# Routing rounds of a mixture of experts: marks as stationary operand, digits streamed, struck keys kept in place

## The chip, the cores and the metric

One Trainium2 chip, one of its cores. The metric is the device time of one execution in microseconds (us), lower is better. TensorE is called PE here (its weight loads are PEld), VectorE DVE, ScalarE ACT, GpSimd POOL, and SP is the engine that issues most DMAs.

## The reference

Three layers follow each other: attention with pooled queries, a capacity-limited mixture of experts, and a gated feed-forward layer. The change lies in the second one, in the step that assigns each of 2304 tokens to one of 8 experts:

```python
def _moe_ref(x, w_gate, w1, w2):
    N, D = x.shape                     # 2304, 512
    E = w_gate.shape[1]                # 8
    cap = N // E                       # 288
    logits = x @ w_gate
    order = np.argsort(-logits.flatten())
    assigned = -np.ones(N, dtype=np.int64)
    counts = np.zeros(E, dtype=np.int64)
    for idx in order:
        tok, e = int(idx) // E, int(idx) % E
        if assigned[tok] >= 0 or counts[e] >= cap:
            continue
        assigned[tok] = e
        counts[e] += 1
    out = np.zeros((N, D), dtype=np.float32)
    for e in range(E):
        mask = assigned == e
        out[mask] = np.maximum(x[mask] @ w1[e], 0.0) @ w2[e]
    return out
```

All pairs of token and expert are taken from the best logit down; a token takes the first expert that still has room.

## The kernel before

The program has four stages, one after the other: attention (up to about 600 us), the rank of every token within every expert (to about 661 us), the routing (661 to 738 us), and the two feed-forward layers, which keep PE busy to the end. The routing needs the ranks and the preferences, and the first expert needs the routing, since its rows of x are gathered by it. So the routing is a serial piece between two stages that are full.

It works in 7 rounds. A token (i, p) lies at partition p and tile i, with NT = 18 tiles of 128. `key` [128, 18, 8] orders the experts of each token, `Ri` holds its rank in each expert's list. A round does this:

- `choose` and `mark`: each token's best expert that is left (`best`, and `dm`, a 0/1 mark for each token and expert).
- The rank of the chosen pair is split in a high digit (0 to 35, GH = 36) and a low digit (0 to 63, GL = 64). `up_to(k)` writes `ths[k]`, a view of `onehot` [128, 36 or 64, 18] in bfloat16 that holds a 1 where the digit is at most the index. It is written in two halves of 9 tiles.
- `count(0, dm)`: 18 matmuls, one for each tile, add up how many chosen tokens have a high digit up to each value, for each expert. The comparison with the capacity `CAP` (288) gives `inh`, and one matmul with ones turns it into the high digit of the cut, spread over all partitions. `at_cut` and `below` compare each token with it.
- `count(1, at_cut)` does the same for the low digit among tokens at the cut, one more matmul adds those below, and `ind` is the comparison. Two matmuls (`mul64` and `ones64`) give the cut as a rank, spread over all partitions.
- `cutb` keeps the lowest cut of each expert so far; the next round's `allowed` compares `Ri` with it (`ok`) and multiplies `key` by that into `s1`, from which the round chooses.

In `count`, the digits are the stationary operand (a slice `ths[k][:, :, i]`, so its columns lie 18 bfloat16 or 36 bytes apart), and the marks are streamed (`who[:, i, :]`, 8 columns side by side); the counts lie by digit, 36 or 64 partitions of 8 values. After a round's last matmul PE transposes four blocks of x for a row tile that ACT scales and SP stores (`rows_after`, six rounds), and then does six matmuls into `acc`, whose result nobody reads (`warm3`, 512 columns each). In this stage the order within an engine is the order of the code, but for what stands under `issue_after`, which waits behind the named instruction. PE, DVE and ACT take their instructions strictly in that order here; a wait is a semaphore.

Of the kernel before, what the change touches and what calls it, by code (L numbers as in the profile page):

```python
# [113 lines left out]
def fused_attention_moe_kernel(ctx: ExitStack, tc: tile.TileContext,  # L114
# [28 lines left out]
    PRM = {'vdue': 6, 'e0': 24, 'egap': 34, 'stag': 6, 'edue': -4, 'rdue': -3, 'plo': -6, 'phi': -8, 'xdue': 3, 'mdue': -10, 'pool': 0, 'vp': (3, 3, 3, 3), 'tok': 1, 'kdue': 2, 'k2due': 2, 'sdue': 0, 'cdue': 40, 'ldma': 1, 'warm': 1, 'warm2': 5, 'warm3': 6, 'nact': (1, 7, 10, 13, 16), 'adel': 2, 'kpref': 5, 'dve': (0, 1, 1, 1), 'edve': (0, 0, 1, 1), 'eat': (1, 4, 7, 9), 'dendue': 10, 'u1due': 0, 'pw': (40, 4, 20, 4), 'tord': 6, 'cmul': 1.35, 'ldlat': 6.0, 'stlat': 6.0, 'eoff': 8, 'espan': 36,  'swn': (3, 3, 3, 3), 'swdue': 2, 'mlo': 2, 'mhi': -8, 'ehold': 16}  # L143
# [1007 lines left out]
    ind = sm("ind", [GL, E], BF)  # L1151
    inh = sm("inh", [GL, E], BF)
    HT = NT // 2

    def choose(src):
        nc.vector.tensor_reduce(best, src, axis=AX.X, op=OP.max)

    def mark(src):
        return nc.vector.tensor_tensor(dm, src, best[:, :, None].to_broadcast([128, NT, E]), op=OP.is_equal)

    def allowed():
        nc.vector.tensor_tensor(ok, Ri, cutb[:, None, :].to_broadcast([128, NT, E]), op=OP.is_lt)
        nc.vector.tensor_mul(s1, ok, key)
        return s1
# [28 lines left out]
    src = key  # L1193
    for rnd in range(E - 1):
        if rnd:
# [5 lines left out]
        p = count(0, dm, GH)  # L1201
# [430 lines left out]
```

## Time and profile before

| | before |
|---|---|
| median of 3 runs | 1428.38 us (1425.8 to 1432.29) |
| the profiled execution | 1425.41 us, of it 1423.6 us from the first to the last instruction |
| PE busy | 1338.2 us, 94% of the span |
| DVE busy | 932.2 us, 65% |
| ACT busy | 612.3 us, 43% |
| POOL busy | 522.6 us, 37% |

The busy shares are means over stages that differ. The routing is some 5% of the span, and PE, which is full before and behind it, has a lower granted clock there. What an edit of the routing is worth is therefore read from one round: which engine each step waits for, and how long.

### The profile page before, as it was taken

The numbers are of one execution on the slowest core, as the hardware profiler recorded it, in microseconds if no ns is written. First come the engines' busy times: TensorE is split into PE (matmuls) and PEld (weight loads), VectorE is DVE, ScalarE is ACT, GpSimd is POOL, SyncE is SP. The second block draws the span as 40 slices with busy tenths as digits, with TensorE's granted clock in tenths as the row PEclk, the third lists the DMA queues.
The fourth block names the chain that finished last, engine by engine and source line by source line (L and its number), as shares of the span: only waits on it lengthen the run. The fifth ranks groups of instructions, "written<-read, shape, count | busy, mean of one in ns | idle before, by whom it ended". The sixth has DMA issues, their size and how long they took to land.

```text
span 1423.6 us, 26934 instructions
## 1 busy us (share of the span) xinstructions
PE 1338.2 (94%) x10278; PEld 1108.9 (78%) x10279; DVE 932.2 (65%) x1940; ACT 612.3 (43%) x1643; POOL 522.6 (37%) x447
## 2 busy tenths in 40 slices
PE   7999999999999888787889999999999999999997
PEld 5666655666665777686669999999999999999997
DVE  5657679878989899878548888866742323232322
ACT  4456555555545565465115555654421212121211
POOL 7545323433324364553027767755610000000000
PEclk9899999999989999887569999999999999999999
DMA  7566566566633886621027767764310101010000
GB/s 221 153 180 182 145 156 184 148 179 190 174 87 87 217 187 158 153 76 53 30 87 239 239 210 254 261 205 128 90 45 1 45 1 45 1 45 1 23 1 23
DMA packets 78353, 174.45 MB, mean 123 GB/s; under 512 B 8448, under 2 KB 38160, under 8 KB 78224
## 3 DMA queue, kind: packets, MB, share of 16 engines
q1 hardware_dynamic: 75248, 163.29, 40.6%
q0 software_dynamic: 2976, 9.44, 1.8%
q8 instruction: 81, 1.33, 0.4%
q14 instruction: 48, 0.39, 0.1%
HBM read 120.86 MB, written 21.31 MB: 100 GB/s over the span
## 4 chain that ended last, share of the span: by engine, by line
PE 61%; issue 17%; DVE 14%; ACT 3%; POOL 2%; DMA 2%; SPq 1%; POOLq 0%; ACTq 0%; DVEq 0%
PE pv L385 8%; PE py L1442 7%; PE ph L1423 7%; PE st L351 6%; DVE cmp L561 5%; PE pg L1529 5%; PE misc L1529 5%; PE po L1552 5%; PE pm L282 4%; PE st L352 3%; PE pv L400 2%; DVE cmp L563 2%; PE pc L1177 2%; PE csum L1224 1%; DVE cmp L993 1%
## 5 line engine op out<-in xcount | busy, mean ns | idle before, releaser
L294 DVE TENSOR_REDUCE mxp<-pm 128x1 f32<-128x384 f32 x405 | 199.6, 549 | 74.4 <-PE pm L282 71.2
L373 ACT ACTIVATE Lrow<-st 128x288 f32<-128x288 f32 (+2 forms) x432 | 154.4, 411 | 95.4 <-PE st L352 82.4
L351 PE MATMUL st<-qs,ks 128*128 128x288 f32 (+2 forms) x504 | 172.7, 354 | 9.8 <-ACT Lrow L373 5.7
L352 PE MATMUL st<-qs,ks 128*128 128x288 f32 (+2 forms) x504 | 150.8, 309 | 3.1 <-ACT qs L333 2.9
L561 DVE SCALAR_TENSOR_TENSOR cmp<-Lrow,Lt,cmp 128x384 fp8e4<-128x384 f32 (+8 forms) x145 | 152.7, 1073 | 0.0
L1560 POOL DMA_INDIRECT out_dram<-ot,si x18 | 17.5, 971 | 362.4 <-DVE ot L1557 359.8
L393 POOL TENSOR_TENSOR Lrow<-Lrow 128x576 f32<-128x576 f32 (+2 forms) x50 | 70.4, 1408 | 204.5 <-ACT Lrow L373 201.9
L1540 DVE TENSOR_TENSOR sg<-pg,sg 128x384 f32<-128x384 f32 x72 | 40.1, 557 | 159.4 <-ACT sg L1539 159.4
L351 PEld LDWEIGHTS st<-qs,ks 128*128 128x128 f32 x504 | 100.0, 198 | 49.3 <-ACT Lrow L373 22.9
L385 PE MATMUL pv<-Lrow,v 128*64 128x288 f32 (+2 forms) x900 | 125.4, 416 | 3.4 <-ACT den L422 3.2
L1339 POOL TENSOR_TENSOR wl<-wr,wh 128x512 fp32r<-128x512 f32 x67 | 104.5, 1567 | 59.8 <-ACT wh L1337 28.9
L352 PEld LDWEIGHTS st<-qs,ks 128*128 128x128 f32 x504 | 101.3, 201 | 4.7 <-ACT qs L333 4.7
L1539 ACT ACTIVATE sg<-pg 128x384 f32<-128x384 f32 x72 | 35.3, 491 | 155.4 <-PE pg L1529 155.4
L1542 ACT CAST ah<-ac 128x384 fp32r<-128x384 f32 x72 | 36.9, 513 | 149.2 <-DVE ac L1541 149.2
L1529 PE MATMUL pg<-yh,w2h 128*128 128x384 f32 x288 | 97.0, 337 | 0.0
L1529 PE MATMUL pg<-yl,w2h 128*128 128x384 f32 x288 | 96.9, 337 | 0.0
L1529 PE MATMUL pg<-yh,w2l 128*128 128x384 f32 x288 | 96.8, 336 | 0.0
L1529 PE MATMUL misc<-yh,w2h 128*128 128x384 f32 x288 | 96.8, 336 | 0.0
L1529 PE MATMUL misc<-yl,w2h 128*128 128x384 f32 x288 | 96.8, 336 | 0.0
L1529 PE MATMUL misc<-yh,w2l 128*128 128x384 f32 x288 | 96.8, 336 | 0.0
L385 PEld LDWEIGHTS pv<-Lrow,v 128*64 128x64 f32 x900 | 59.4, 140 | 46.8 <-issue 13.8
L1552 PE MATMUL po<-w2l,ah 128*128 128x512 f32 x216 | 85.5, 396 | 0.0
(285 smaller groups left out, 3490.2 us busy)
## 6 DMA issues: line engine op xcount, KB each, us to landing
wr<-in_wm_dram SPq DMA_DIRECT2D x64, 512.0 KB, 3.6
raw<-in_wm_dram SPq DMA_DIRECT2D x36, 512.0 KB, 4.5
ks<-pkh SPq DMA_DIRECT2D x23, 576.0 KB, 5.6
v<-in_v_dram SPq DMA_DIRECT2D x20, 576.0 KB, 6.3
pk<-in_kT_dram SPq DMA_DIRECT2D x16, 576.0 KB, 5.3
pq<-in_qT_dram SPq DMA_DIRECT2D x32, 288.0 KB, 5.8
Lrow<-l_cols SPq DMA_DIRECT2D x18, 512.0 KB, 5.4
ks<-kh_s SPq DMA_DIRECT2D x16, 576.0 KB, 7.0
```

What stands on the lines that cost most here:

```text
L294: nc.vector.tensor_reduce(mx[:, i, j:j + 1], p[:, :w3], axis=AX.X, op=OP.max)
L351: nc.tensor.matmul(p[:, :w], KS[u][:, 1, ks], QS[u][:, 1, cs_], start=True, stop=False)
L352: nc.tensor.matmul(p[:, :w], KS[u][:, 0, ks], QS[u][:, 0, cs_], start=False, stop=True)
L373: nc.scalar.activation(EX[u, gi, kt][:, ti * w:(ti + 1) * w], ST.pop((u, gi, kt, ti))[:, :w], AF.Exp, scale=SCALE)
L385: nc.tensor.matmul(p[64 * k:64 * k + 64, :hn], VT[u][:, kt, o:o + 64], ex[:, k * hn:(k + 1) * hn], start=(kt == 0), stop=(kt == KT - 1), s ...
L393: nc.gpsimd.tensor_add(w[:, :n], a, b)
L561: nc.vector.scalar_tensor_tensor(c[:, sl], Lrow[:, e, sl], Lt[:, i, e:e + 1], c[:, sl], op0=OP.is_ge, op1=OP.add, accum_out=acc, saturate= ...
L1339: eng.tensor_sub(WL[k][:, s], r[:, s], WH[k][:, s].bitcast(F32))
L1423: nc.tensor.matmul(p[:, :CAP], w[:, cs_], x[:, c, :], start=(n == 0), stop=(n == 11))
L1442: nc.tensor.matmul(PY[e][m][:, :CAP], w[:, ms], h, start=(f == 0 and n == 0), stop=(f == FB1 - 1 and n == 2))
L1529: nc.tensor.matmul(p[:, :TG], w[ft][:, cs_], y[g][:, c, :], start=(n == 0), stop=(n == 11))
L1552: nc.tensor.matmul(PO[g][t], a[:, ts], w[ft][:, 1024:], start=(ft == 0 and n == 0), stop=(ft == FB2 - 1 and n == 2))
```

## The change

The edit has these parts, all in the rounds:

- In `count` the operands change places: the marks (8 columns) are loaded as weights, and the digits (36 or 64 columns, 36 bytes apart) are streamed. The counts then lie by expert, 8 partitions of 36 or 64 values.
- `cut` takes the place of the single comparisons `inh` and `ind`: one DVE instruction compares with the capacity and adds up along the row (`accum_out`), a second spreads the sum along 128 columns (`pick`). The matmul that spreads the cut over the partitions has `pick` as weights and a unit matrix of 8 by 8 (times 64 for the high digit) as moving operand.
- `cutb`, `s1` and `allowed` go. A round ends with `ok`, which reads the cut where the matmul left it, and `key` is multiplied by `ok` in place.
- The six matmuls `warm3` of each round go.

```diff
-    def allowed():
-        nc.vector.tensor_tensor(ok, Ri, cutb[:, None, :].to_broadcast([128, NT, E]), op=OP.is_lt)
-        nc.vector.tensor_mul(s1, ok, key)
-        return s1
...
-    def count(k, who, n):
+    def count(k, who):
         p = pmx2.tile([128, 512], F32, name="pc")
+        n = (GH, GL)[k]
         for i in range(NT):
-            nc.tensor.matmul(p[:n, :E], ths[k][:, :, i], who[:, i, :], start=(i == 0), stop=(k == 0 and i == NT - 1))
+            nc.tensor.matmul(p[:E, :n], who[:, i, :], ths[k][:, :, i], start=(i == 0), stop=(k == 0 and i == NT - 1))
         return p
+    def cut(k, p):
+        n = (GH, GL)[k]
+        nc.vector.scalar_tensor_tensor(under[:, :n], p[:E, :n], float(CAP), onesb[:E, :n], op0=OP.is_le,
+                                       op1=OP.mult, accum_out=cuts[k])
+        return nc.vector.tensor_scalar(pick[k], onesb[:E], cuts[k], None, op0=OP.mult)
...
-        ins = nc.vector.tensor_scalar(inh[:GH], p[:GH, :E], float(CAP), None, op0=OP.is_le)
+        ins = cut(0, p)
         with tc.issue_after(ins.ins):
             up_to(1, (1,))
         p = pmx2.tile([128, 512], F32, name="pc")
-        nc.tensor.matmul(p[:, :E], ones64[:GH], inh[:GH], start=True, stop=True)
+        nc.tensor.matmul(p[:, :E], pick[0], unit8[0], start=True, stop=True)
...
-        p = count(1, at_cut, GL)
-        nc.tensor.matmul(p[:GL, :E], onesb[:, :GL], nbelow, start=False, stop=True)
-        nc.vector.tensor_scalar(ind, p[:GL, :E], float(CAP), None, op0=OP.is_le)
+        p = count(1, at_cut)
+        nc.tensor.matmul(p[:E, :GL], nbelow, onesb[:, :GL], start=False, stop=True)
+        cut(1, p)
         p = pmx2.tile([128, 512], F32, name="pc")
-        nc.tensor.matmul(p[:, :E], mul64[:GH], inh[:GH], start=True, stop=False)
-        mm = nc.tensor.matmul(p[:, :E], ones64, ind, start=False, stop=True)
+        nc.tensor.matmul(p[:, :E], pick[0], unit8[1], start=True, stop=False)
+        mm = nc.tensor.matmul(p[:, :E], pick[1], unit8[0], start=False, stop=True)
         rows_after(mm)
-        with tc.issue_after(mm.ins):
-            for _ in range(PRM["warm3"]):
-                nc.tensor.matmul(acc, ident8f, small.bitcast(F8)[:, :512], start=True, stop=True)
-        nc.vector.tensor_tensor(cutb, cutb, p[:, :E], op=OP.min)
-    src = allowed()
-    choose(src)
-    mark(src)
+        nc.vector.tensor_tensor(ok, Ri, p[:, None, :E].to_broadcast([128, NT, E]), op=OP.is_lt)
+        nc.vector.tensor_mul(key, key, ok)
+    choose(key)
+    mark(key)
```

On PE, the rows from the last count of a round to the first of the next stand so before (the stationary operand is named on LDWEIGHTS, and `small` and `ident8f` belong to the matmuls that nobody reads, of which one of six is shown):

```order
L1177 MATMUL pc<-at_cut,onehot 64x8
L1219 LDWEIGHTS mul_8467
L1219 MATMUL pc<-inh,mul_8467 128x8
L1216 LDWEIGHTS onesb
L1216 MATMUL pc<-nbelow,onesb 64x8
L1220 LDWEIGHTS onesb
L1220 MATMUL pc<-ind,onesb 128x8
L500 MATMUL misc<-identf,xT 128x128 x4
L1224 LDWEIGHTS ident8f
L1224 MATMUL csum<-small,ident8f 128x512
```

and so in the changed kernel (its lines are numbered anew):

```order
L1171 MATMUL pc<-onehot,at_cut 8x64
L1214 LDWEIGHTS nbelow
L1214 MATMUL pc<-onesb,nbelow 8x64
L1217 LDWEIGHTS pick_8491
L1217 MATMUL pc<-unit_8493,pick_8491 128x8
L1218 LDWEIGHTS pick_8492
L1218 MATMUL pc<-identb,pick_8492 128x8
L500 MATMUL misc<-identf,xT 128x128 x4
L1171 LDWEIGHTS dm
L1171 MATMUL pc<-onehot,dm 8x36
```

The matmul of the high digit now stands behind that of `nbelow`, the weights of the two spreading matmuls are what DVE has just written, and the next count follows the transposes directly.

On DVE, the rows from the end of one round to the first comparison of the next stand so before:

```order
L1217 TENSOR_SCALAR ind<-pc 64x8
L1225 TENSOR_TENSOR cutb<-cutb,pc 128x8
L1162 TENSOR_TENSOR ok<-Ri,cutb 128x144
L1163 TENSOR_TENSOR s_8483<-ok,key 128x144
L1156 TENSOR_REDUCE best<-s_8483 128x18
L1198 TENSOR_SCALAR dig_8487<-best 128x18
L1159 TENSOR_TENSOR dm<-s_8483,best 128x144
L1171 TENSOR_TENSOR onehot<-colv,dig_8487 128x36x9 x2
L1202 TENSOR_SCALAR dig_8488<-best 128x18
L1203 SCALAR_TENSOR_TENSOR hd<-dm,high 128x144
L1171 TENSOR_TENSOR onehot<-colv,dig_8488 128x64x9
L1205 TENSOR_SCALAR inh<-pc 36x8
```

and so in the changed kernel:

```order
L1177 SCALAR_TENSOR_TENSOR under,cut_8490<-pc,onesb 8x64
L1179 TENSOR_SCALAR pick_8492<-onesb,cut_8490 8x128
L1220 TENSOR_TENSOR ok<-Ri,pc 128x144
L1221 TENSOR_TENSOR key<-key,ok 128x144
L1153 TENSOR_REDUCE best<-key 128x18
L1196 TENSOR_SCALAR dig_8482<-best 128x18
L1156 TENSOR_TENSOR dm<-key,best 128x144
L1163 TENSOR_TENSOR onehot<-colv,dig_8482 128x36x9 x2
L1200 TENSOR_SCALAR dig_8483<-best 128x18
L1201 SCALAR_TENSOR_TENSOR hd<-dm,high 128x144
L1163 TENSOR_TENSOR onehot<-colv,dig_8483 128x64x9
L1177 SCALAR_TENSOR_TENSOR under,cut_8489<-pc,onesb 8x36
```

Two instructions stand where `ind` (and, a row further, `inh`) stood alone, and `cutb` is gone. The order on ACT, POOL and SP is the same in both programs.

## Rows read from the trace of the kernel before

**Rows 1.** The chain that ended last, in one round: start, length, work.

```profile
706.89 2.56 PE csum L1224 x6
```

**Rows 2.** Timeline of PE over the rounds: start, length, line, output<-inputs.

```profile
671.21 0.16 PE L1220 MATMUL pc<-ind,onesb 64*128 64x8 bf16 x1 [0.25 <-DVE ind L1217]
...
709.38 1.40 PE L1177 MATMUL pc<-dm,onehot 128*36 128x8 bf16 x18
...
711.68 2.21 PE L1177 MATMUL pc<-at_cut,onehot 128*64 128x8 bf16 x18 [0.50 <-DVE at_cut L1211]
713.82 0.18 PE L1219 MATMUL pc<-inh,mul 36*128 36x8 bf16 x1
...
722.79 0.16 PE L1220 MATMUL pc<-ind,onesb 64*128 64x8 bf16 x1 [0.25 <-DVE ind L1217]
```

**Rows 3.** Timeline of DVE in the round from 705.7 to 714.4.

```profile
705.88 0.16 DVE L1225 TENSOR_TENSOR cutb<-cutb,pc 128x8 int16<-128x8 int16 x1 [0.25 <-PE pc L1220]
706.07 0.23 DVE L1162 TENSOR_TENSOR ok<-Ri,cutb 128x144 bf16<-128x144 int16 x1
...
707.32 0.40 DVE L1171 TENSOR_TENSOR onehot<-colv,dig 128x324 bf16<-128x324 int16 x1
...
710.82 0.16 DVE L1205 TENSOR_SCALAR inh<-pc 36x8 bf16<-36x8 f32 x1 [2.09 <-PE pc L1177]
710.90 0.58 DVE L1171 TENSOR_TENSOR onehot<-colv,dig 128x576 bf16<-128x576 int16 x1
711.35 0.28 DVE L1211 TENSOR_TENSOR at_cut<-hd,pc 128x144 bf16<-128x144 bf16 x1
...
714.18 0.16 DVE L1217 TENSOR_SCALAR ind<-pc 64x8 bf16<-64x8 f32 x1 [1.89 <-PE pc L1216]
```

**Rows 4.** Timeline of PE's weight loads: strided weights of 36, 64 and 128 columns.

```profile
709.38 1.31 PEld L1177 LDWEIGHTS <-onehot 128*36 128x36 bf16 x18 [0.84 <-DVE onehot L1171]
...
711.68 2.11 PEld L1177 LDWEIGHTS <-onehot 128*64 128x64 bf16 x17 [0.38 <-issue]
...
730.52 1.15 PEld L1286 LDWEIGHTS <-onehot 128*128 128x128 f16 x17 [0.99 <-issue]
```

**Rows 5.** Weight loads grouped by shape, 661 to 740 us: busy us, mean ns of one.

```profile
L1177 PEld LDWEIGHTS <-onehot 128*64 128x64 bf16 x126 | 16.2, 215 | 4.8 <-issue 4.8
L1177 PEld LDWEIGHTS <-onehot 128*36 128x36 bf16 x126 | 9.3, 165 | 12.1 <-DVE onehot L1171 11.5 <-DVE dig L1202 0.6
...
L1286 PEld LDWEIGHTS <-onehot 128*128 128x128 f16 x54 | 4.0, 164 | 3.0 <-DVE onehot L1272 1.8 <-issue 1.0
...
L1216 PEld LDWEIGHTS <-onesb 128*64 128x64 bf16 x7 | 0.9, 126 | 0.1
```

**Rows 6.** DVE sums of 144 values grouped by shape, 661 to 740 us.

```profile
L1214 DVE TENSOR_REDUCE nbelow<-below 128x8 bf16<-128x144 bf16 x7 | 2.9, 413 | 0.2
...
L1264 DVE TENSOR_REDUCE slot<-dr 128x18 int16<-128x144 f32 x2 | 0.6, 303 | 0.1
```

**Rows 7.** Timeline of PE behind the last round: products with columns side by side.

```profile
725.67 0.51 PE L1249 MATMUL pc<-dm,onesb 128*128 128x120 bf16 x5
726.02 0.28 PE L1249 MATMUL pc<-dsum,onesb 128*128 128x96 bf16 x2
```

**Rows 8.** Timeline of DVE at the end of the attention: a comparison with its sum.

```profile
586.79 0.34 DVE L563 SCALAR_TENSOR_TENSOR cmp<-Lrow,Lt,tri 128x128 fp8e4<-128x128 f32 x1
587.07 0.08 DVE L563 DVE_READ_ACCUMULATOR cmp<-Lrow,Lt,tri 128x1 f32 x1
```

**Rows 9.** A DVE instruction of 128 bfloat16 columns, grouped by shape.

```profile
L588 DVE TENSOR_TENSOR eq<-eq,low 128x128 bf16<-128x128 bf16 x1 | 0.2, 198 | 0.0
```

**Rows 10.** Windows from the first expert on: busy us (x instructions) of PE, PEld, DVE, ACT, POOL; granted clock.

```profile
738.20:741.10 2.90, 2.90 (x11) 2.69 (x12) 1.52 (x4) 0.84 (x3) 2.24 (x3) 0.50 0.36 96
741.10:760.00 18.90, 18.90 (x140) 18.41 (x139) 13.00 (x19) 10.42 (x22) 12.48 (x9) 1.00 0.47 148
760.00:1400.00 640.00, 637.94 (x3768) 603.78 (x3767) 329.71 (x523) 218.80 (x450) 201.94 (x154) 1.00 0.30 98
```

More of the change, by code (lines that the diff above doesn't have):

```diff
@@ L142, in fused_attention_moe_kernel @@
     BUFS = {'st': 3, 'pm': 4, 'cmp': 8, 'ex': 6, 'pv': 1, 'ks': 2, 'sw': 2}
-    PRM = {'vdue': 6, 'e0': 24, 'egap': 34, 'stag': 6, 'edue': -4, 'rdue': -3, 'plo': -6, 'phi': -8, 'xdue': 3, 'mdue': -10, 'pool': 0, 'vp': (3, 3, 3, 3), 'tok': 1, 'kdue': 2, 'k2due': 2, 'sdue': 0, 'cdue': 40, 'ldma': 1, 'warm': 1, 'warm2': 5, 'warm3': 6, 'nact': (1, 7, 10, 13, 16), 'adel': 2, 'kpref': 5, 'dve': (0, 1, 1, 1), 'edve': (0, 0, 1, 1), 'eat': (1, 4, 7, 9), 'dendue': 10, 'u1due': 0, 'pw': (40, 4, 20, 4), 'tord': 6, 'cmul': 1.35, 'ldlat': 6.0, 'stlat': 6.0, 'eoff': 8, 'espan': 36,  'swn': (3, 3, 3, 3), 'swdue': 2, 'mlo': 2, 'mhi': -8, 'ehold': 16}
+    PRM = {'vdue': 6, 'e0': 24, 'egap': 34, 'stag': 6, 'edue': -4, 'rdue': -3, 'plo': -6, 'phi': -8, 'xdue': 3, 'mdue': -10, 'pool': 0, 'vp': (3, 3, 3, 3), 'tok': 1, 'kdue': 2, 'k2due': 2, 'sdue': 0, 'cdue': 40, 'ldma': 1, 'warm': 1, 'warm2': 5, 'nact': (1, 7, 10, 13, 16), 'adel': 2, 'kpref': 5, 'dve': (0, 1, 1, 1), 'edve': (0, 0, 1, 1), 'eat': (1, 4, 7, 9), 'dendue': 10, 'u1due': 0, 'pw': (40, 4, 20, 4), 'tord': 6, 'cmul': 1.35, 'ldlat': 6.0, 'stlat': 6.0, 'eoff': 8, 'espan': 36,  'swn': (3, 3, 3, 3), 'swdue': 2, 'mlo': 2, 'mhi': -8, 'ehold': 16}
     cst = ctx.enter_context(tc.tile_pool(name="cst", bufs=1))
@@ L1111, in fused_attention_moe_kernel @@
     pref(last, rst)
-    ones64 = onesb[:64]
-    mul64 = rst.tile([64, 128], BF, name="mul64")
-    nc.vector.memset(mul64, 64.0)
     after.close()
@@ L1136, in fused_attention_moe_kernel @@
     nc.vector.tensor_scalar(high, high, float(GL), None, op0=OP.add)
-    cutb = sm("cutb", [128, E], I16)
-    nc.vector.memset(cutb, N)
     ok = sm("ok", [128, NT, E], BF)
-    s1 = sm("s1", [128, NT, E])
     best = sm("best", [128, NT])
@@ L1150, in fused_attention_moe_kernel @@
     nbelow = sm("nbelow", [128, E], BF)
-    ind = sm("ind", [GL, E], BF)
-    inh = sm("inh", [GL, E], BF)
+    under = sm("under", [E, GL], BF)
+    cuts = [sm(f"cut{k}", [E, 1]) for k in range(2)]
+    pick = [sm(f"pick{k}", [E, 128], BF) for k in range(2)]
+    unit8 = [identb[:E, :E], sm("unit64", [E, E], BF)]
+    nc.vector.tensor_scalar(unit8[1], identb[:E, :E], float(GL), None, op0=OP.mult)
     HT = NT // 2
@@ L1189, in rows_after @@
             tok_store(i)
-    src = key
     for rnd in range(E - 1):
-        if rnd:
-            src = allowed()
-        choose(src)
+        choose(key)
         nc.vector.tensor_scalar(digs[0], rnk, 6, None, op0=OP.logical_shift_right)
-        mark(src)
+        mark(key)
         up_to(0)
-        p = count(0, dm, GH)
+        p = count(0, dm)
         nc.vector.tensor_scalar(digs[1], rnk, GL - 1, None, op0=OP.bitwise_and)
@@ L1214, in fused_attention_moe_kernel @@
             nc.vector.tensor_reduce(nbelow, below.rearrange("p i e -> p e i"), axis=AX.X, op=OP.add)
-        p = count(1, at_cut, GL)
-        nc.tensor.matmul(p[:GL, :E], onesb[:, :GL], nbelow, start=False, stop=True)
-        nc.vector.tensor_scalar(ind, p[:GL, :E], float(CAP), None, op0=OP.is_le)
+        p = count(1, at_cut)
+        nc.tensor.matmul(p[:E, :GL], nbelow, onesb[:, :GL], start=False, stop=True)
+        cut(1, p)
         p = pmx2.tile([128, 512], F32, name="pc")
-        nc.tensor.matmul(p[:, :E], mul64[:GH], inh[:GH], start=True, stop=False)
-        mm = nc.tensor.matmul(p[:, :E], ones64, ind, start=False, stop=True)
+        nc.tensor.matmul(p[:, :E], pick[0], unit8[1], start=True, stop=False)
+        mm = nc.tensor.matmul(p[:, :E], pick[1], unit8[0], start=False, stop=True)
         rows_after(mm)
-        with tc.issue_after(mm.ins):
-            for _ in range(PRM["warm3"]):
-                nc.tensor.matmul(acc, ident8f, small.bitcast(F8)[:, :512], start=True, stop=True)
-        nc.vector.tensor_tensor(cutb, cutb, p[:, :E], op=OP.min)
-    src = allowed()
-    choose(src)
-    mark(src)
+        nc.vector.tensor_tensor(ok, Ri, p[:, None, :E].to_broadcast([128, NT, E]), op=OP.is_lt)
+        nc.vector.tensor_mul(key, key, ok)
+    choose(key)
+    mark(key)
     assert not rows_left
```

## The prediction

> **What bounds the kernel now.** I read the chain of waits first. In each of the seven rounds it goes once around PE and DVE, and it contains the six matmuls `csum` that nobody reads [rows 1]. PE and DVE therefore set the length of a round in turn, and whatever leaves this circle shortens the program, if the stage behind it passes the gain on. It should: from 760 to 1400 us PE is busy for 637.9 of 640 us [rows 10], and its loads of weights are released by PE's own progress, so the whole stage moves forward.
>
> The round itself I read from the timelines of PE and DVE. The last matmul of the first round starts at 671.21 and that of the seventh at 722.79 [rows 2], so six rounds take 51.58 us, 8.60 us each. One round has four legs. From the first product of `count(0)` (709.38) to the comparison `inh` (710.82) it takes 1.44 us; from there to the first product of `count(1)` (711.68) 0.86 us; from there to the comparison `ind` (714.18) 2.50 us [rows 2, 3]. `ind` takes 0.16 us, and a step from DVE to PE 0.05 us (`at_cut` ends at 711.63, its product starts at 711.68) [rows 2, 3], together 0.21 us to the round's last matmul, which I call T. What is left of 8.60 us, 3.59 us, lies between T and the next `count(0)`.
>
> That leg has a wait in it. From T to `cutb` it takes 0.20 us (a product of 0.16 us [rows 2] and 0.04 us to DVE), from `cutb` to the first half of the digits 1.44 us (705.88 to 707.32), and that half takes 0.40 us [rows 3]. With 0.05 us to PE the count could start 2.09 us after T. It starts at 3.59: PE is still in its useless products, and **1.50 us of each round is waiting for them**.
>
> **Term 1, `warm3` and `cutb` go.** Without the six products the count starts when the digits are there. DVE also loses `cutb` (0.19 us from its start to that of `ok` [rows 3]); `ok` now reads the cut from PSUM and should take 0.28 us as `at_cut` does, not 0.23 [rows 3], +0.05; a load of 128 columns that has to wait for `pick` adds about 0.02 (bounds: nothing, since the load of 709.38 and its product start together [rows 2, 4], and 0.13 us, the length of a load that lies side by side [rows 5]). The leg becomes 2.09 - 0.19 + 0.05 + 0.02 = 1.97 us: **-1.62 us in each of the six rounds that have a round ahead**. The transposes that stay behind T end about 1.2 us after it (`csum` follows them at 706.89 [rows 1], and T is 0.20 ahead of the 705.88 of `cutb` [rows 3]), ahead of the digits.
>
> **Term 2, the operands of `count` change places.** The pace of loads and products is set by the loads: 18 of 36 columns span 1.31 us with 0.165 for one, so (1.31 - 0.165)/17 = 67.4 ns each; 17 of 64 columns give (2.11 - 0.215)/16 = 118.4 ns [rows 4, 5]. Between the two lie 28 columns and 51 ns, **1.82 ns a column**, with 2 ns left over. The same 64 columns lying side by side load in 126 ns in all, against 215 [rows 5]. So the cost is that of columns 36 bytes apart. DVE shows nearly the same price: a sum over 144 values 16 bytes apart takes 413 ns, over 144 neighbours 303 [rows 6], 0.76 ns more for each value, on another engine. I take 1.82 ns as the price of a separate place in the memory, whoever reads it. The changed count streams exactly these columns: 36 x 1.82 and 64 x 1.82 again, with the load of 8 neighbouring marks hidden behind. **The swap alone is worth nothing.** Bounds: 0.83 ns a column and 10 ns for each product, as for streams side by side (five products of 120, 96, 72, 48 and 24 columns in 726.02 - 725.67 = 0.35 us [rows 7]), and 2.9 ns from above (below).
>
> One row speaks against this: loads of 128 strided columns go at (1.15 - 0.164)/16 = 62 ns [rows 4, 5], less than 64 columns take. The Trainium skill's "TensorE: Matmul & The Clock Gate", section "Weight-path perf modes", says that a full load of 128 columns that is not float32 is split into four chunks read side by side; 32 x 1.82 + 2 = 60 ns is then what one chunk takes, and the trace agrees. Without that page one could read the row as 0.48 ns a strided column, and the swap would gain as in rival A. The Trainium skill's "SBUF — State Buffer", section "Door 1: The DMA port swizzle", adds that each access to a new 16-byte line pays a penalty, which would hold for streamed columns too; no row here shows a stream with such steps that is long enough to tell.
>
> The order of the short products gains a little. From `inh`'s product (713.82) to `ind` (714.18) it takes 0.36 us [rows 2, 3], where the one product that `ind` needs, of 64 columns in the changed kernel, takes 0.21 us (0.16 for 8, and 56 more at 0.83 ns) and the step to DVE 0.04. `inh`'s product now stands behind it, off the path: **-0.10 us a round**.
>
> **Term 3, `cut` is two instructions with a sum between.** A comparison with its sum is followed by a read of the accumulator of 0.08 us, which starts 0.06 us before the end of the 0.34 us of 128 columns and ends 0.02 us behind it [rows 8]. With 36 or 64 columns in place of 8 the comparison takes 0.19 or 0.22 us (0.16 for 8 [rows 3], 0.34 for 128 [rows 8]). Then a step on DVE of 0.04 us, `pick` of 128 bfloat16 columns at 0.20 us (the nearest row, [rows 9]; bounds 0.16 and 0.34), and 0.05 to PE. For the low digit: 0.22 + 0.02 + 0.04 + 0.20 + 0.05 = 0.53 against 0.21, **+0.32 us**. For the high digit `at_cut` waits for the second half of the low digits, which stand behind the comparison now as before: that half starts 0.08 us after `inh` and `at_cut` 0.45 us later [rows 3]. Behind `pick` it starts 0.19 + 0.02 + 0.04 + 0.20 - 0.08 = 0.37 us after the comparison, 0.29 later than now: **+0.29 us**, and it covers the product in between (0.50 + 0.18 + 0.04 = 0.72, against 0.82). Bounds for both together: 0.42 (all at 0.16) and 1.0 us (0.34 and 0.29).
>
> **The end.** Behind the seventh T the useless products delay those of L1249, which end at 726.02 + 0.28 = 726.30, 3.51 us after T [rows 2, 7]. Without them the marks are ready about 1.52 us after T (where the digits start in other rounds, 1.97 - 0.45), then 0.05 to PE, 0.12 for a product of 144 columns, 0.35 and 0.28 as now [rows 7]: 2.32 us, **-1.19 us**.
>
> **The sum.** A round behind another: -1.62 - 0.10 + 0.32 + 0.29 = -1.11 us, six times -6.7. The first round has only the new costs, +0.5. The end gives -1.2. Together **-7.3 us**. The profiled execution took 1425.41 us (a span of 1423.6 and 1.8 around it), 3 us below the median; its 1418.1 correspond to 1421.1 at the median of 1428.38. With the bounds of term 3 the sum runs from -8.6 to -4.6; with the scatter of a median of few runs the likeliest case has 1418 to 1425.
>
> **Rivals.**
>
> A. Streams at full pace. If streaming does not mind the 36 bytes, 36 columns take 36 x 0.83 + 10 = 40 ns and 64 take 63 ns [rows 7], and each round gains 17 x (67.4 - 40) + 17 x (118.4 - 63) = 1.41 us more, 9.9 us in all: 1411.2 us. For it, the Trainium skill's "TensorE: Matmul & The Clock Gate", section "Back-to-back issue gap", gives the columns divided by 1.2 at the low clock, whatever their distance, an estimate of 30 and 53 ns; it has the same rule for loads, where the trace disagrees with 67 and 118. Against A: the two engines' agreement on 1.8 ns. Chance 0.15.
>
> B. Streams slower than the loads, the case that ends on the other side. The only streamed strided columns of the trace, 21 of them, hide behind loads of 62 ns [rows 4], so up to 2.9 ns a column would not show. A round streams 17 x (36 + 64) columns behind its first ones, seven rounds 11,900; 2.9 ns would cost 11,900 x 1.08 = 12.9 us, total +5.6, 1434.0 us. It outweighs the rest above 1.82 + 7.3/11.9 = 2.43 ns a column. Chance 0.05.
>
> C. The products were not useless: they kept PE busy. The first expert starts at 738.20 and for 2.90 us has the granted clock of 0.50 (1.2 GHz), 11 products; then, at 1.00, 140 in 18.9 us [rows 10], 0.264 against 0.135 us each. If the clock rises later, each us costs half a us; as late again (2.9 us) would cost 1.4 us: 1422.5. Against it: the clock of 0.50 stood there although the products of the seventh round ran until L1249 began (725.43, 0.24 ahead of [rows 7]). Chance 0.06.
>
> **How the numbers follow.** The forecast's chance is 0.74. The range of 1411 to 1427 us takes in A's centre, the bounds of term 3 and the scatter of single runs (1425.8 to 1432.3 before), and leaves B out. About 0.5% (7.1 us) can be told from no change, and my sum stands next to it: of 0.74 I count 0.38 as faster, with A and a little of C 0.54; same 0.42; slower 0.04 (most of B).
>
> **What would show it.** Right: the loads of `count` no longer set the pace, the products stand 67 and 118 ns apart; the count starts 2.0 us after T; rounds of 7.5 us; two DVE instructions and an accumulator read of 0.45 us in all between the count and the cut. Wrong: products 40 and 63 ns apart (A) or over 120 (B); a clock that rises more than 3 us into the first expert (C); a gap on DVE between the comparison and `pick`; or PE waiting more behind 760 us than today's 2 us of 640, if the loads of weights were what sets that stage.

## The result and the profile after

The changed kernel takes 1415.82 us (median of 8 runs, 1414.76 to 1424.65) against 1428.53 for the kernel before in the same comparison: a ratio of 0.9919, with a 95% interval of 0.9891 to 0.9947. A second comparison, on another occasion, gave 0.9944 (0.9924 to 0.9964). The profiled execution took 1414.83 us, its span is 1413.0 us; that of before 1423.6.

The timeline of PE over one round of the changed kernel and over the end of the last round answers to [rows 2] and [rows 7] (start, length, line, output<-inputs, what the idle time before waited for):

```profile
692.83 0.18 PE L1218 MATMUL pc<-identb,pick 8*128 8x8 bf16 x1 [0.48 <-DVE pick L1179]
692.94 1.11 PE L500 MATMUL misc<-identf,xT 128*128 128x128 f32 x4
694.82 1.36 PE L1171 MATMUL pc<-onehot,dm 128*8 128x36 bf16 x18 [0.77 <-DVE onehot L1163]
696.74 0.18 PE L1207 MATMUL pc<-identb,pick 8*128 8x8 bf16 x1 [0.56 <-DVE pick L1179]
697.40 2.26 PE L1171 MATMUL pc<-onehot,at_cut 128*8 128x64 bf16 x18 [0.47 <-DVE at_cut L1209]
...
700.31 0.18 PE L1218 MATMUL pc<-identb,pick 8*128 8x8 bf16 x1 [0.48 <-DVE pick L1179]
...
715.26 0.18 PE L1218 MATMUL pc<-identb,pick 8*128 8x8 bf16 x1
...
717.30 0.28 PE L1244 MATMUL pc<-dsum,onesb 128*128 128x96 bf16 x2
```

The round's last matmul T stands at 692.83 and at 700.31: a round takes 7.48 us where it took 8.60 [rows 2]. Behind T only the four transposes are left on PE, and then PE waits for the digits; the products of [rows 1] are gone from the circle. The last round's T is at 715.26, and the slots' products end at 717.58.

The timeline of DVE in the same round answers to [rows 3]:

```profile
694.37 0.66 DVE L1163 TENSOR_TENSOR onehot<-colv,dig 128x324 bf16<-128x324 int16 x2
...
696.22 0.18 DVE L1177 SCALAR_TENSOR_TENSOR under<-pc,onesb 8x36 bf16<-8x36 f32 x1 [0.45 <-PE pc L1171]
696.34 0.07 DVE L1177 DVE_READ_ACCUMULATOR under<-pc,onesb 8x1 f32 x1
696.44 0.24 DVE L1179 TENSOR_SCALAR pick<-onesb,cut 8x128 bf16<-8x128 bf16 x1
696.61 0.58 DVE L1163 TENSOR_TENSOR onehot<-colv,dig 128x576 bf16<-128x576 int16 x1
697.07 0.28 DVE L1209 TENSOR_TENSOR at_cut<-hd,pc 128x144 bf16<-128x144 bf16 x1
...
699.75 0.21 DVE L1177 SCALAR_TENSOR_TENSOR under<-pc,onesb 8x64 bf16<-8x64 f32 x1 [1.74 <-PE pc L1214]
699.90 0.07 DVE L1177 DVE_READ_ACCUMULATOR under<-pc,onesb 8x1 f32 x1
700.01 0.24 DVE L1179 TENSOR_SCALAR pick<-onesb,cut 8x128 bf16<-8x128 bf16 x1
700.53 0.30 DVE L1220 TENSOR_TENSOR ok<-Ri,pc 128x144 bf16<-128x144 int16 x1 [0.28 <-PE pc L1218]
```

Where one comparison stood there are now three entries: comparison, accumulator read, `pick`. Behind the count of the low digit they take from 699.75 to 700.25, and the round's last matmul waits for all of it.

The view of the line of the products in the changed kernel gives their lengths (min/median/max in ns, first and last start in us):

```profile
L1171 PE MATMUL pc<-onehot,dm x126: 224/246/247, 664.2 to 710.9; 128*8 128x36 bf16 x126
...
L1171 PE MATMUL pc<-onehot,at_cut x126: 274/296/298, 667.5 to 714.3; 128*8 128x64 bf16 x126
```

With them 18 products of 36 columns are (1.36 - 0.246)/17 = 65.5 ns apart and 18 of 64 columns (2.26 - 0.296)/17 = 115.5, in the way that the loads gave 67.4 and 118.4 [rows 4, 5]. Between 36 and 64 columns that is 1.79 ns for each streamed column.

The windows of the stage behind, which answer to [rows 10] (busy us and instructions of PE, PEld, DVE, ACT, POOL, then the granted clock):

```profile
728.70:729.70 1.00, 0.87 (x4) 0.65 (x5) 0.98 (x3) 0.90 (x3) 0.93 (x1) 0.98 0.00 0
729.70:733.10 3.40, 3.40 (x16) 3.40 (x15) 1.03 (x3) 0.41 (x1) 1.81 (x2) 0.50 0.59 163
...
760.00:1390.00 630.00, 627.89 (x3706) 594.01 (x3705) 324.27 (x511) 213.23 (x439) 196.44 (x150) 1.00 0.29 96
```

PE is as full as before, 627.9 of 630 us, so the stage has moved forward as a whole. The first expert starts at 728.74 here, so its first us still has the high clock, and the low one lasts from 729.7 to 733.1.

The five stretches of a program, each worked out from the starts of rows in PE's timeline, show where the 10.6 us between the two spans lie. C is the first product of the first count, S the end of the slots' products, X the first product of the first expert, Y the last product on that line; all in us from the first instruction. The other kernels are those of the experiments.

| kernel | C | C to S | S to X | X to Y | Y to the end |
|---|---|---|---|---|---|
| before | 665.5 | 60.8 | 11.9 | 223.4 | 462.0 |
| before, again | 672.6 | 61.4 | 11.9 | 222.7 | 462.0 |
| after | 664.2 | 53.4 | 11.2 | 222.3 | 462.1 |
| after, again | 667.6 | 53.4 | 11.8 | 222.4 | 462.0 |
| before without products | 666.0 | 51.0 | 11.9 | 223.2 | 462.0 |
| after with products | 667.9 | 64.8 | 11.8 | 222.9 | 462.0 |
| after without the swap | 663.3 | 50.1 | 11.8 | 223.0 | 462.4 |
| after, digits side by side | 663.8 | 46.7 | 11.3 | 222.2 | 462.0 |
| no swap, digits side by side | 670.9 | 43.1 | 11.8 | 223.0 | 462.3 |
| the same, whole table | 669.7 | 43.1 | 11.9 | 222.9 | 462.4 |
| the same, written apart | 664.8 | 81.3 | 12.0 | 223.0 | 462.4 |

The change lies in C to S: 60.8 to 53.4, 7.4 us less, in a second pair of profiles 61.4 to 53.4. The other 3 us of the first pair are in the other columns, and the sections below ask whether they belong to the change. Read in steps, C to S goes from 60.8 to 51.0 when the products go (experiment 1), to 50.1 when `cutb` goes too and the key is struck out in place (experiment 5), and back up to 53.4 with the swap and its cut in two steps: -9.8, -0.9 and +3.3 us.

### The profile page after: what moved, and what is told of

It is laid out like the page before. It is cut to its first block, busy times and chain, and to the rows that moved or that the text cites. A ratio compares the mean times of both kernels' runs of the same rounds, so it can differ in the third digit from the quotient of the medians.

```text
span 1413.0 us, 26870 instructions
## 1 busy us (share of the span) xinstructions
PE 1318.2 (93%) x10236; PEld 1095.4 (78%) x10237; DVE 938.4 (66%) x1960; ACT 612.5 (43%) x1643; POOL 520.8 (37%) x447
## 4 chain that ended last, share of the span: by engine, by line
PE 54%; DVE 18%; issue 17%; ACT 4%; POOL 2%; DMA 2%; SPq 1%; POOLq 0%; ACTq 0%; DVEq 0%
PE pv L385 8%; PE py L1437 7%; PE ph L1418 7%; PE st L351 6%; DVE cmp L561 6%; PE pm L282 4%; PE pg L1524 4%; PE misc L1524 4%; PE po L1547 4%; PE st L352 3%; PE pv L400 2%; DVE cmp L563 2%; PE pc L1171 2%; DVE cmp L993 1%; DVE mxp L294 1%
## 5 line engine op out<-in xcount | busy, mean ns | idle before, releaser
L385 PEld LDWEIGHTS pv<-Lrow,v 128*64 128x64 f32 x900 | 59.2, 140 | 46.7 <-issue 13.6
```

The source lines that it names most:

```text
L385: nc.tensor.matmul(p[64 * k:64 * k + 64, :hn], VT[u][:, kt, o:o + 64], ex[:, k * hn:(k + 1) * hn], start=(kt == 0), stop=(kt == KT - 1), s ...
```

## The experiments

**1. Before without products.** Does the gain come from the products that went?

```diff
-    PRM = {... 'warm2': 5, 'warm3': 6, ...}
+    PRM = {... 'warm2': 5, 'warm3': 0, ...}
```

> The kernel before with the six useless products of each round left out and nothing else changed. My theory (the products are the gain; the swap of the operands is worth nothing and the two-step cut costs 0.6 us a round): the first product of the next count starts 2.09 us after the round's last product instead of 3.59, rounds of 7.10 us, and with 1.19 us at the end 10.2 us less than before, about 1418 us: more than the sum of 7.3 us forecast for the whole change. Rival S (the gain comes from the swapped operands): within 2 us of the time before. Rival C (the products kept PE's clock up): the rounds get shorter, but the clock rises more than 3 us into the first expert and the time is less than 9 us below before.

1416.15 us, ratio 0.9929 (0.9904 to 0.9954), 10.1 us below before. The timeline of PE:

```profile
693.18 0.16 PE L1220 MATMUL pc<-ind,onesb 64*128 64x8 bf16 x1 [0.25 <-DVE ind L1217]
693.27 1.12 PE L500 MATMUL misc<-identf,xT 128*128 128x128 f32 x4
695.28 1.40 PE L1177 MATMUL pc<-dm,onehot 128*36 128x8 bf16 x18 [0.89 <-DVE onehot L1171]
```

The count starts 2.10 us after T and waits for the digits. C to S is 51.0 us, 9.8 less than before and 2.4 less than in the changed kernel. In C to S, one number in the table of parameters gives more than the whole change (the whole times, at 0.9929 against 0.9919 and 0.9944, don't tell the two apart): rival S is out. Of the two signs of rival C one came: the clock rose 6.0 us into the first expert. The other did not, since the time is not less than 9 us below before. The part on the prediction comes back to this.

**2. After with the products put back.** The swap, the cut in two steps and the key in place alone.

```diff
+        with tc.issue_after(mm.ins):
+            for _ in range(PRM["warm3"]):
+                nc.tensor.matmul(acc, ident8f, small.bitcast(F8)[:, :512], start=True, stop=True)
         nc.vector.tensor_tensor(ok, Ri, p[:, None, :E].to_broadcast([128, NT, E]), op=OP.is_lt)
```

> The changed kernel with the six products put back behind each round's last product: the swap, the two-step cut and the key in place alone. My theory: the count starts 3.6 us after the last product again, rounds of about 9.1 us (7.48 measured and 1.6 more), and the time is 3 to 4 us over that of before, about 1432 us. Rival S (the gain comes from the swap): 8 us or more below before. If the 3 us that the two profiles show outside the rounds and the tail came with the swap and not with the run, 1429 us.

1430.56 us, ratio 1.0017 (1.0002 to 1.0032), 2.4 us over before by the ratio and 3.3 by the medians, where 3 to 4 were expected. The timeline of PE:

```profile
692.49 0.18 PE L1218 MATMUL pc<-identb,pick 8*128 8x8 bf16 x1 [0.48 <-DVE pick L1179]
692.60 1.11 PE L500 MATMUL misc<-identf,xT 128*128 128x128 f32 x4
693.50 2.77 PE L1222 MATMUL csum<-small,ident8f 128*128 128x512 fp8e4 x6
696.20 1.36 PE L1171 MATMUL pc<-onehot,dm 128*8 128x36 bf16 x18
...
701.68 0.18 PE L1218 MATMUL pc<-identb,pick 8*128 8x8 bf16 x1 [0.48 <-DVE pick L1179]
```

The count stands behind the products again, 3.71 us after T, and a round takes 9.19 us. C to S is 3.9 us longer than in the first profile of before and 3.4 longer than in the second: taken together, all that the change does beside removing the products is a loss.

**3. After with the digits side by side.** Is it the distance that sets the products' pace?

```diff
-    ths = [onehot[:, :GH], onehot[:, GH:GH + GL]]
+    ths = [junk[:, NT * a:NT * b].rearrange("p (i n) -> p i n", i=NT) for a, b in ((0, GH), (GH, GH + GL))]
...
-            nc.vector.tensor_tensor(ths[k][:, :, sl], grid[:, :n, sl],
-                                    digs[k][:, None, sl].to_broadcast([128, n, HT]), op=OP.is_ge)
+            nc.vector.tensor_tensor(ths[k][:, sl], vals[:, None, :n].to_broadcast([128, HT, n]),
+                                    digs[k][:, sl, None].to_broadcast([128, HT, n]), op=OP.is_ge)
...
-            nc.tensor.matmul(p[:E, :n], who[:, i, :], ths[k][:, :, i], start=(i == 0), stop=(k == 0 and i == NT - 1))
+            nc.tensor.matmul(p[:E, :n], who[:, i, :], ths[k][:, i], start=(i == 0), stop=(k == 0 and i == NT - 1))
```

`junk` is the same memory as `onehot`, in one row; `vals` is a new row of 64 numbers.

> The changed kernel with the digits of a token column side by side in memory (18 times 36 and 18 times 64) instead of 36 bytes apart; the comparison that writes them reads one row of values and the digits, both repeated. My theory (1.8 ns for each column that lies apart, loaded or streamed): the products stand 40 and 63 ns apart, or about 62 if a load of 8 marks has a least pace of that, so 1.0 to 1.4 us less a round and 7 to 10 us less than the changed kernel in all, 1406 to 1409 us. Rival P (the pace comes from the pair of a load and a product, not from the distance): 67 and 116 ns as now, no change from the changed kernel. The two halves of the digits on DVE should take 0.40 and 0.59 us as now; if they mind the new operands, the difference is lost there.

1410.58 us, ratio 0.9889 (0.9864 to 0.9914). The timeline of PE:

```profile
690.76 0.84 PE L1172 MATMUL pc<-onehot,dm 128*8 128x36 bf16 x18 [0.85 <-DVE onehot L1164]
...
693.39 1.12 PE L1172 MATMUL pc<-onehot,at_cut 128*8 128x64 bf16 x18 [0.69 <-DVE at_cut L1210]
```

The view of the line of these products (min/median/max ns of one):

```profile
L1172 PEld LDWEIGHTS <-at_cut x126: 83/112/112, 667.5 to 707.2; 128*8 128x8 bf16 x126
L1172 PE MATMUL pc<-onehot,at_cut x126: 213/242/242, 667.5 to 707.2; 128*8 128x64 bf16 x126
```

The timeline of DVE, the high digit's two halves and the low digit's first:

```profile
690.22 0.90 DVE L1164 TENSOR_TENSOR onehot<-vals,dig 128x324 bf16<-128x324 int16 x2
...
691.33 0.75 DVE L1164 TENSOR_TENSOR onehot<-vals,dig 128x576 bf16<-128x576 int16 x1
```

Products of 64 neighbouring columns are (1.12 - 0.242)/17 = 51.6 ns apart, 0.81 ns a column, against 115.5 at 36 bytes, at the same granted clock of 0.50 in both (1.2 GHz). Rival P falls. The load of eight marks sets no floor of 62 ns, and the 63 ns of the expectation were too many: the 10 ns for each product are not there. The Trainium skill's "TensorE: Matmul & The Clock Gate", section "Back-to-back issue gap", gives N/1.2 for 64 columns at the low clock, 53 ns: the trace agrees for neighbours and disagrees for columns 36 bytes apart. C to S is 6.7 us shorter than in the changed kernel, a little less than the 7 to 10 that were expected, and the time misses the expected 1406 to 1409 us. The trace shows where the rest is lost: DVE does mind. Its two halves of the low digit take 0.75 us each, not 0.58, and the second half of the high digit now ends while PE counts the first.

**4. No swap, no products, digits side by side.** The fastest combination by the sum.

```diff
-            nc.tensor.matmul(p[:E, :n], who[:, i, :], ths[k][:, i], start=(i == 0), stop=(k == 0 and i == NT - 1))
+            nc.tensor.matmul(p[:n, :E], ths[k][:, i], who[:, i, :], start=(i == 0), stop=(k == 0 and i == NT - 1))
...
-        ins = cut(0, p)
+        ins = nc.vector.tensor_scalar(inh[:GH], p[:GH, :E], float(CAP), None, op0=OP.is_le)
...
-        cut(1, p)
+        nc.vector.tensor_scalar(ind, p[:GL, :E], float(CAP), None, op0=OP.is_le)
...
```

The short products behind the counts are those of before as well; the edit is shown against experiment 3.

> The operands of the count as before (digits loaded, marks streamed, one comparison between the count and the cut), without the useless products, with the key struck out in place, and with the digits side by side in memory. My theory: loads of 36 and 64 neighbouring columns go at 62 ns or less, the leg from comparison to product is 0.3 us shorter at each digit than in the changed kernel, so rounds of 5.9 to 6.1 us and 18 to 21 us below before, 1408 to 1410 us by the sum, 3 to 4 us below the changed kernel with digits side by side. Rival S (the swap is the gain): slower than that one by 5 us or more.

1409.44 us, ratio 0.9857 (0.9831 to 0.9882), 20.4 us below before. The timeline of PEld:

```profile
692.19 0.98 PEld L1170 LDWEIGHTS <-onehot 128*64 128x64 bf16 x17 [0.67 <-issue]
```

The timeline of DVE around the comparison of the high digit:

```profile
690.44 0.75 DVE L1164 TENSOR_TENSOR onehot<-vals,dig 128x576 bf16<-128x576 int16 x1
691.11 0.15 DVE L1195 TENSOR_SCALAR inh<-pc 36x8 bf16<-36x8 f32 x1
691.18 0.74 DVE L1164 TENSOR_TENSOR onehot<-vals,dig 128x576 bf16<-128x576 int16 x1
691.85 0.29 DVE L1201 TENSOR_TENSOR at_cut<-hd,pc 128x144 bf16<-128x144 bf16 x1
```

Loads of 64 neighbours go 17 in 0.98 us, where 17 at 36 bytes took 2.11 [rows 4]: the price of distance is the same in either place. A round takes 5.97 us. C to S is 3.6 us below the swapped kernel with the same digits, as expected; the medians differ by 1.1 us. It beats both kernels of this case. A wait has also changed sides: `inh` no longer waits for PE; the half of the low digits in front of it ends later than the count.

**5. After without the swap.** Experiment 4 with the digits 36 bytes apart; `ths` and `up_to` are those of before.

```diff
-            nc.tensor.matmul(p[:n, :E], ths[k][:, i], who[:, i, :], start=(i == 0), stop=(k == 0 and i == NT - 1))
+            nc.tensor.matmul(p[:n, :E], ths[k][:, :, i], who[:, i, :], start=(i == 0), stop=(k == 0 and i == NT - 1))
...
```

> The changed kernel without the swap and the two-step cut: digits loaded and marks streamed as before, one comparison between the count and the cut; the useless products gone and the key struck out in place, digits 36 bytes apart. My theory (swap worth nothing, the two-step cut costs 0.65 us a round, the order of the short products gives 0.10 back): 3 to 4 us below the changed kernel, rounds of about 7.0 us against 7.48, 1 us below the kernel before without products, about 1417 us where before is 1428. Rival S (the swap is a gain): slower than the changed kernel. Rival K (the swapped count raises PE's clock ahead of the first expert, which gives the cut back): equal to the changed kernel, with the difference behind the tail.

1412.81 us, ratio 0.9892 (0.9876 to 0.9908), against 0.9944 (0.9924 to 0.9964) for the changed kernel in the same comparison. The timeline of PE:

```profile
704.04 0.16 PE L1209 MATMUL pc<-ind,onesb 64*128 64x8 bf16 x1 [0.25 <-DVE ind L1206]
706.01 1.40 PE L1169 MATMUL pc<-dm,onehot 128*36 128x8 bf16 x18 [0.77 <-DVE onehot L1163]
711.05 0.16 PE L1209 MATMUL pc<-ind,onesb 64*128 64x8 bf16 x1 [0.25 <-DVE ind L1206]
```

Rounds of 7.01 us, C to S 3.3 us below the changed kernel: as expected, and the cost of the swap with its two-step cut. The medians differ by 6.6 us, twice that, and 1412.81 lies 4 us below the 1417 that were expected; the two profiled runs differ by 6.7, of which 3.3 lie in C to S and 4.3 ahead of C (663.3 against 667.6), ahead of all rounds, less 1.0 behind S. Rivals S and K fall: behind S this kernel is slower by 1.0 us and not by the 3.3 (11.8, 223.0 and 462.4 against 11.8, 222.4 and 462.0). Why the four kernels without the swap and without `cutb` take 0.3 to 0.4 us more from Y to the end stays open.

**6 and 7. After and before again.** Unchanged copies, for second profiles.

> The changed kernel itself, for a second profile and for a direct comparison with the kernel without the swap. From the first product of the first count to the end of the slots' products its profile took 53.4 us and that of before 60.8; this repeats within 0.2 us. If the 3 us that the first profiles differ outside this stretch (1.3 ahead, 0.7 and 1.2 behind) are where the clock happens to fall in a run, they come out otherwise here, by 1 us or more; if they belong to the change, they stay: 11.2 us from the slots' products to the first expert (11.9 before), 222.2 from there to the last expert's first half (223.4 before).

> The kernel before itself, for a second profile. First count to slots' products 60.8 us again within 0.2. If the differences outside belong to the run: 11.9 and 223.4 us behind it change by half a us or more, and the time to the first count by 1 us or more; if to the kernel, they stay.

The changed kernel had 1419.45 us (ratio 0.9944), before 1426.14 (0.9991, 0.9970 to 1.0011). C to S came out as 53.4 us again for the changed kernel, within 0.02 us; for before 61.4, 0.6 more and outside the 0.2 that I allowed. In the first profile three of its rounds had been shorter (8.57, 8.47 and 8.40 us, where the others and nearly all of the second profile have 8.7); the granted clock had been up in stretches of these. In the second profile it was up as well (682.6 to 686.0, for one), but in other parts of the rounds. Windows in two of the three, in the first profile of before:

```profile
684.00:686.00 2.00, 1.26 (x17) 1.29 (x16) 1.05 (x5) 0.00 (x0) 0.00 (x0) 1.00 0.24 91
701.00:703.00 2.00, 1.26 (x19) 1.29 (x17) 0.91 (x4) 0.00 (x0) 0.00 (x0) 1.00 0.34 131
```

What lies outside C to S is not the kernel's: C moved by 7.1 us between two profiles of before and by 3.4 between two of after, and over all kernels it lies between 663.3 and 672.6 with no order by what was changed. The 0.7 us from S to X did not come back in the second profile of after (11.8). X to Y was 222.3 and 222.4 in after, 223.4 and 222.7 in before. By the rules set ahead of these runs that leaves it open, since it moved by 0.7 us in before and by no more than 0.2 in after.

The granted clock in the traces tells more. In the first profile of before it fell once more behind the start of the first expert (a window of that profile):

```profile
833.40:836.80 3.40, 3.40 (x17) 3.40 (x16) 3.40 (x4) 1.11 (x3) 3.40 (x3) 0.51 0.65 224
```

Added up between X and Y, PE had the low clock for 6.5 us in the first profile of before (223.4 us in all), 5.0 in the second (222.7), 3.4 in after (222.3) and 4.3 in its second profile (222.4). Over all eleven profiles X to Y grows by 0.38 us with each us at the low clock (correlation 0.98). Ahead of C the time at the low clock goes from 68 to 87 us, and C grows by 0.48 us with each (correlation 0.91, single profiles up to 2.3 us off the line), with no order by what was changed. So what lies outside C to S goes with where the clock fell in a run.

**8. No swap, digits side by side, whole table of values.** Why is DVE slower there?

```diff
-            nc.vector.tensor_tensor(ths[k][:, sl], vals[:, None, :n].to_broadcast([128, HT, n]),
+            nc.vector.tensor_tensor(ths[k][:, sl], vals[:, sl, :n],
```

> The fastest kernel of the first four runs (operands as before, no products, key in place, digits side by side) with a whole table of values side by side for the comparison that writes the digits, in place of one row repeated. There the two halves of the digits took 0.48 and 0.74 us, in the changed kernel 0.40 and 0.585. If the repeated row is what slows DVE, they come down to 0.40 and 0.59 and a round from 5.97 to about 5.7 us, 2 us in all; if it is the repeated digits or the way of writing, they stay at 0.48 and 0.74 and nothing changes.

1410.53 us, ratio 0.9877 (0.9855 to 0.9898). DVE grouped by shape (busy us, mean ns of one):

```profile
L1164 DVE TENSOR_TENSOR onehot<-vals,dig 128x576 bf16<-128x576 int16 x6 | 4.5, 746 | 0.0
L1164 DVE TENSOR_TENSOR onehot<-vals,dig 128x324 bf16<-128x324 int16 x4 | 1.8, 490 | 0.0
```

Nothing changed, rounds of 5.97 us again: the repeated row of values was not the cause of the 0.16 us more that a half of 576 takes here.

**9. The same digits, written in the old order.** The reads of before, the results 72 and 128 bytes apart.

```diff
-            nc.vector.tensor_tensor(ths[k][:, :, sl], grid[:, :n, sl],
+            nc.vector.tensor_tensor(ths[k][:, sl].rearrange("p i n -> p n i"), grid[:, :n, sl],
                                     digs[k][:, None, sl].to_broadcast([128, n, HT]), op=OP.is_ge)
```

> The kernel without the swap and with digits side by side, but written by DVE in the order of the kernel before (one digit value after another, tokens within), so that neighbouring results go to places 72 and 128 bytes apart; the reads are those of before. If the repeated digits within the run are what made the two halves 0.49 and 0.745 us, they come back to 0.40 and 0.585 and the round goes from 5.97 to about 5.7 us, 2 us in all. If DVE pays for results that lie apart as its sums pay for operands that lie apart (0.76 ns each), 0.65 and 1.02 us, and rounds of 6.3 to 6.5 us, 3 us slower than with neighbouring results.

1450.15 us, ratio 1.0167 (1.0146 to 1.0188). DVE grouped by shape:

```profile
L1163 DVE TENSOR_TENSOR onehot<-colv,dig 128x576 bf16<-128x576 int16 x4 | 10.7, 2840 | 0.0
L1163 DVE TENSOR_TENSOR onehot<-colv,dig 128x324 bf16<-128x324 int16 x5 | 7.6, 1681 | 0.0
...
L1191 DVE TENSOR_SCALAR dig<-best 128x18 int16<-128x18 int16 x2 | 0.8, 392 | 0.0
```

Both expectations miss. A half of 576 results takes 2.84 us, 4.9 ns a result, and the short instruction that starts as a half ends takes 0.39 us where it took 0.17 in experiment 4. It is the direction that was expected of the second theory, and the half is nearly three times as long as it expected; rounds are 11.63 us, and C to S is 38 us longer than in experiment 4, where 3 were expected. The reads are those of experiment 5, whose half of 576 takes 0.59 us: the writing alone makes the rest. Whether the 0.16 us in experiments 3, 4 and 8 come from the digits repeated within a run is left open, since this kernel changed the writing too.

## Why the prediction was right

The forecast was 1421.1 us in a range of 1411 to 1427, with a sum of -7.3 us; the result is 1415.82, and the part that the sum speaks of, C to S, measured -7.4 and, against the second profile of before, -8.0 us. The mechanism was right term by term; that the median fell 5 us below the forecast was not foreseen (the last paragraph of this part). By its own steps, from the rows of after above:

- **Term 1** (1.97 us from T to the count, -1.62 in a round): 692.83 to 694.82, 1.99 us. Experiment 1 shows that it is the waiting for the products that went: -9.8 us of C to S without touching anything else (-10.4 against the second profile of before), where 10.2 was forecast for it.
- **Term 2** (the swap is worth nothing): 65.5 and 115.5 ns where the loads had 67.4 and 118.4. Rivals A (40 and 63 ns) and B (over 120) are out. Experiments 3 and 4 show what the prediction could only argue: it is the distance of the columns, for a load as for a stream, since both come down to 52 to 54 ns for 64 neighbours (loads: (0.98 - 0.12)/16). The prediction's own support for it was weaker than it reads. The two DVE sums of [rows 6] differ in type and in the number of results too, and 0.76 ns more a value is not an agreement on 1.8 ns (the like excess on PE is 1.0 ns). The order of the short products: the leg from the count of the low digit to its comparison takes 699.75 - 697.40 = 2.35 us, -0.15 where -0.10 was forecast.
- **Term 3** (+0.32 and +0.29 us): from the comparison of the low digit to T 0.56 us against 0.21, +0.35; from that of the high digit to the next count 1.18 against 0.86, +0.32. `pick` takes 0.24 us, not 0.20, and that is the miss. `ok` takes 0.30, not 0.28. The lower bound was added up wrongly: with all at 0.16 us the two legs give 0.22 each, 0.44 and not 0.42, and the sum's lower end would be -8.5.
- **The end** (2.32 us from T to the end of the slots' products): 715.26 to 717.58, 2.32 us.
- **The sum of a round**: 7.48 us where 8.60 - 1.11 = 7.49 was forecast.

**Rival C** was argued with a sentence that held in part only: that the granted clock of 0.50 stood there although the products ran. In stretches it was 1.00 (the windows of experiment 7). The three profiles with the products have such stretches in the rounds (both of before, and experiment 2), the eight without them have 0.50 all through. So the products did raise the clock, and it bought next to nothing: a round that held such a stretch was up to 0.3 us shorter, or no shorter at all. The reason stands in the rows. A count of before at a clock of 1.00 takes the 1.40 us that it takes at 0.50 [rows 2] (timeline of PE, and the window of that count):

```profile
717.78 1.40 PE L1177 MATMUL pc<-dm,onehot 128*36 128x8 bf16 x18
717.78:719.18 1.40, 1.40 (x19) 1.38 (x19) 0.00 (x0) 0.00 (x0) 0.00 (x0) 1.00 1.01 395
```

and with the digits streamed, in experiment 2, a count that is at 1.00 for all but its last 0.3 us takes the 2.26 us that it takes in after at 0.50:

```profile
689.58 2.26 PE L1171 MATMUL pc<-onehot,at_cut 128*8 128x64 bf16 x18 [0.48 <-DVE at_cut L1209]
689.58:691.50 1.92, 1.92 (x17) 1.75 (x18) 0.57 (x2) 0.00 (x0) 0.00 (x0) 1.00 0.00 0
```

The products' stretches did not carry over to the first expert either. The clock rose 2.9 us into it in before [rows 10], 5.0 us in the second profile of before, 4.4 us in after (of which 3.4 at the low clock) and 6.0 us in before without products. So the sign that the prediction gave for C, a rise more than 3 us into the first expert, came true, but it can't tell: a second run of the kernel before shows it too. The windows of the second profile of before:

```profile
745.90:750.90 5.00, 5.00 (x20) 4.80 (x21) 1.95 (x5) 1.24 (x4) 2.79 (x3) 0.51 0.44 120
750.90:756.00 5.10, 5.10 (x40) 5.10 (x40) 1.15 (x2) 3.69 (x8) 2.76 (x3) 1.00 0.07 15
```

From X to Y the kernels with products take 222.7 to 223.4 us and those without 222.2 to 223.2, so no loss of the size of C (1.4 us) is there. The other signs of being wrong did not come: the step from the comparison to `pick` is 0.05 us on DVE, and PE waits 2 us behind 760 as before.

**What the sum did not hold**: 5 us between the forecast and the median, of which the terms explain next to nothing. The first pair of profiles differs by 1.3 us ahead of C, by 0.7 from S to X and by 1.2 from X to Y; the second pair by 5.0, 0.0 and 0.3. The ratio of the second comparison gives 8.0 us (1427.71 x 0.0056) in place of 11.6 from the first (1428.53 x 0.0081), and 8.0 is what C to S of the second pair shows. Runs with a lower granted clock are longer: of eight runs of before, again, the fastest has 1421.1 us at a mean clock of 0.953 and the slowest 1433.3 at 0.943. With the times at the low clock in the eleven profiles (experiments 6 and 7) I count the extra as the scatter of where the clock falls, mostly ahead of C. That the differences go with the clock is shown; no run set the clock by itself, and what decides where it falls stays open. The first comparison's median was this much better than the sum by luck, within the range that had been left for it.

## What to carry to other kernels

When a change does several things, price each alone: here the products that went did nearly all the good (9.8 us), and the swap with its cut in two steps gave a third of it back (3.3 us), which the total hid. Columns that lie 36 bytes apart cost TensorE the same here whether they are loaded or streamed; changing places moves the cost, and putting neighbours side by side removes most of it, if the engine that writes them can write side by side too. A serial piece ahead of a full stage passed on what it saved here (from S to the end all eleven profiles lie within 2 us of each other), so work put there to keep an engine busy must be shown to buy something: these products did raise the clock, for counts whose pace does not follow the clock. The stage ahead is less full than the start of this text has it (PE is busy for 50.7 of the 61 us from 600 to 661), but a gain needs only the stage behind to be full.

## What the runs showed of the hardware that was not expected

- **Writing apart is far dearer than reading apart.** DVE took 4.9 ns for a result when neighbouring bfloat16 results go 128 bytes apart (2.84 us for 576; 72 bytes, 1.68 us for 324, gave 5.2), against 1.0 ns with the same reads and results in runs of nine neighbours (0.59 us, experiment 5) and 1.3 ns with all side by side (0.745 us). Reading 16 bytes apart cost DVE 0.76 ns more a value [rows 6], in rows that differ in type and results too, and 36 bytes cost PE 1.0 ns more a column (1.79 against 0.81, at a clock of 0.50). The Trainium skill's "SBUF — State Buffer", section "Door 1: The DMA port swizzle", says that every access to a new 16-byte line pays a penalty, without a figure; all three agree in direction.
- **A load of 8 columns is no limit** on products behind each other: in experiment 3 its row reads 112 ns at the median, and the products stand 51.6 ns apart.
- **The granted clock does not set the pace of columns 36 bytes apart.** Counts take 1.40 us (36 columns loaded) and 2.26 us (64 streamed) at a granted clock of 0.50 and of 1.00 alike, where the products of the first expert go from 0.264 to 0.135 us each [rows 10]. So the clock rose in stretches of the rounds of before, with PE's products behind each round, and still such a round was at most 0.3 us shorter (8.40 against 8.71 us).
